# A fused attention, MLP and soft mixture of experts: g turned by VectorE in 32x32 blocks, and the sum over tokens taken from 32x32 array tiles into four partial sums

## The chip, the cores and the metric

The kernel runs on one core of a Trainium2 chip. The metric is the time of one execution on the device in microseconds (us), less being better. The kernel before was timed three times: 657.53, 661.55 and 662.04 us, median 661.55. One more execution was profiled; all rows below are from that one.

TensorE does the matmuls, VectorE (DVE), ScalarE (ACT) and GpSimd (POOL) the elementwise work, and SyncE (SP) issues the DMA transfers.

## The reference

Causal attention over 4 batches of 12 heads (448 tokens, head size 64), then an MLP with a gate, then a soft mixture of experts over all 1792 tokens:

```python
scores = np.where(mask, -1e9, scale * q @ k.T)
attn = exp(scores - max) / sum
x = (attn @ v)                       # 1792 x 768
h = x @ w_in                         # 1792 x 2048
g = h * np.clip(h + 3.0, 0.0, 6.0) / 6.0
y = g @ w_out                        # 1792 x 768
logits = y @ phi                     # 1792 x 32
d = softmax over the tokens of logits
slot_input = d.T @ y                 # 32 x 768, 8 experts x 4 slots
slot_out[e] = np.maximum(slot_input[e] @ w1[e], 0.0) @ w2[e]
out = softmax over the slots of logits @ slot_out
```

## The kernel before

The kernel never forms y. It folds w_out and phi into one matrix wp (2048 x 32), so that the logits come from g, and it takes the slot inputs as U times w_out, where U is the sum over tokens of z (the exponentials of the logits, 32 slots) times g.

Attention runs over 24 pairs of heads, six to a batch. A pair has first score matmuls for the maxima (L473, in two parts, with mask matmuls L479), the maxima on VectorE (L488 and L492), a small matrix from them (the diagonal, L502 to L506, on POOL or VectorE), the masked matmuls into PSUM (L523 and L528, two parts), the exponentials on ScalarE (L538), and the product with v (L561). Both kinds of scores take their PSUM buffers from one pool, "ps".

The MLP's hidden layer is done in f-tiles of 128 features: for each batch 16 groups of 18 matmuls (L731), with the weights prepared by L717 and L720. ScalarE forms the gate (L736) and VectorE multiplies (L738), which gives g with features on the partitions, 128 x 448. The logits take it as it is (L760 and L779). The sum over tokens needs the tokens on the partitions, so TensorE transposes each f-tile of g in four pieces (L745) and ScalarE copies them into the tile gtok in two (L750 and L752). When a batch is complete, its z is transposed (L871; of the last batch L807) and 16 matmuls with K = 128 tokens, M = 32 slots and N = 512 features form its part of U on four column tiles of the array (L889; of the last batch L831, in four quarters), and VectorE adds it to U with the factor by which the running maximum has changed (L900, L837).

After the last batch, U is transposed (L994, L996) and multiplied with w_out (L1004), the slot inputs go through selb (L1021), and eight experts' weights w1 and w2 (64 loads of 768 KB into buffers of a pool called ring, and into parts of the tile wos) are used as they arrive (L1051 and on). Last, the combine and the output.

The order of all instructions is worked out by a planner (class Schedule) from costs, priorities and the buffers of each pool that are free. In a pool outside of SHARED, buffers are handed out in the order in which the code asked for them; in a SHARED one (here "t" and "h") whoever is ready takes one. Each engine then runs its list in order. The weights' ring buffers appear step by step, when earlier memory is given back: cv_end, a_end, b_end, x_end, h_end (after the last hidden group), g_end (after every user of the pools "g", "r" and "ls"), m_end, o_end (after the slot inputs' last matmul). Table RINGS says how many buffers each step adds. SyncE has one list for all of this, so a load that waits holds the ones behind it.

Of the kernel before, what the change touches and what calls it, by code (L numbers as in the profile page):

```python
# [19 lines left out]
TU = {'PO': [-6.32, -14.01, -12.03, 3.38], 'TO': [-7.42, -13.26, 43.39, 23.92], 'PB': 0.63, 'AB': -1.38, 'TB': 194.0, 'DUTY': 0.6, 'RINGS': [2, 4, 2, 3, 1, 6, 2, 3], 'LOOK': 0.49, 'FILL': 0.96, 'RAW': 3, 'CA': 1, 'CW': 1, 'S': 2, 'PAIR': 13.04, 'UNIT': 5.54, 'WP0': 36.34, 'WPS': 13.71, 'T0': 215.5, 'L0': 24.86, 'L1': 5.94, 'GP': 198.33, 'TP': 5.85, 'ZP': 54.85, 'UP': 15.88, 'P0': 15.72, 'NQ': 2, 'WAIT': 0.09, 'AHEAD': 2.19, 'LAT': 0.23, 'CX': 2, 'G': 5, 'R': 1, 'VR': 2, 'XT': 2, 'Q': 1, 'AS': 1.42, 'A1': -6.49, 'A2': 8.66, 'A3': 15.93, 'A4': -8.97, 'A5': 11.2, 'A6': 28.01, 'A7': 15.62, 'DG': 2, 'DV': 6, 'TT': 2, 'LO': 5.3, 'DA': 6, 'DX': 6}  # L20
# [17 lines left out]
class Schedule:  # L38
# [4 lines left out]
    LAT = 0.15  # L43
# [8 lines left out]
    SHARED = ("t", "h")  # L52
# [14 lines left out]
    def buf(self, name):  # L67
        b = Buf(name)
        self.queue.setdefault(name, []).append(b)
        return b  # L70
# [17 lines left out]
    def ready_at(self, s):  # L88
        t = max([d.end + self.LATS.get(d.eng, 0.0) for d in s.deps], default=0.0)
        need = {}  # L90
        for b in s.use:
            if b.t is None:
                if b.pool not in self.SHARED and self.queue[b.pool][0] is not b:
                    return None
                need[b.pool] = need.get(b.pool, 0) + 1
# [22 lines left out]
    def run(self):  # L118
# [8 lines left out]
        while todo:  # L127
# [28 lines left out]
            for b in s.use:  # L156
                if b.t is None:
                    fr = min(self.free[b.pool], key=lambda x: x[:2])
                    self.free[b.pool].remove(fr)
                    self.queue[b.pool].remove(b)  # L160
# [25 lines left out]
def kernel(  # L186
# [81 lines left out]
    with tc.manual_schedule():  # L268
# [58 lines left out]
        sc.pool("zt", [zt])  # L327
# [362 lines left out]
        SM, SNM, SAL, SSUM, SB, SMN = 0, 1, 2, 3, 4, 5  # L690
# [9 lines left out]
        for b in range(B):  # L700
# [5 lines left out]
            for ft in range(KF):  # L706
# [34 lines left out]
                tp = sc.buf("t")  # L741
# [12 lines left out]
                a = sc.add("PE", 0.47, tr, [gg], [tp, g, gtb], pr - TU["TP"])  # L754
                a.weight = 0.35
                lasts.append(sc.add("ACT", 0.75, ev, [a], [tp, gtb], pr - TU["GP"]))
                if ft == KF - 3 if fin and ft > KF - 4 else ft % 4 == 3:
# [9 lines left out]
                    ll = sc.add("PE", 0.9, lg, gts[-nx:] + [wp_done[ft // 4]], [L] + gs[-nx:], pr - TU["TP"])  # L767
            pr = T0 + UNIT * KF - TU["ZP"]
# [6 lines left out]
            if fin:  # L775
# [465 lines left out]
```

## Time and profile before

| | |
|---|---|
| median of three runs | 661.55 us |
| profiled execution, span | 659.1 us |
| TensorE busy | 608.8 us (92%), 5800 instructions |
| VectorE busy | 391.5 us (59%) |
| ScalarE busy | 281.7 us (43%) |
| POOL busy | 144.9 us (22%) |
| moved by DMA | 144.57 MB, mean 219 GB/s |

The profile gives each instruction's start and duration, by line of the kernel. Busy time over the whole span says little here, since the kernel has stages with different limits; it has to be read by stretch. The chain that ended last is followed back from the last instruction through what released each one. Instructions of TensorE are pipelined, so that a single duration is longer than the distance between two. A matmul of 32-bit operands appears as two instructions in the trace.

### The profile page before, as it was taken

To read this page: it belongs to the slowest core of one execution; us is meant where nothing else is said; L and a number is where in the kernel's file an instruction comes from. 1 tells how busy PE (TensorE), PEld (TensorE's weight loads), DVE (VectorE), ACT (ScalarE), POOL (GpSimd) and SP (SyncE) were. 2 spreads that over 40 slices of the span, in tenths; PEclk is the share of its full clock that TensorE was granted. 3 is DMA by queue.
4 is the path that set the end of the run, shared out by engine and by line. 5 is a ranking of instruction groups with operands and counts; after the bars stand their busy time and mean duration, and the time that the engine had idled before them with its cause. 6 is when DMAs were issued, how large, how long until landed. Compare 5 with 4: busy or idle time off the path is not lost.

```text
span 659.1 us, 14610 instructions
## 1 busy us (share of the span) xinstructions
PE 608.8 (92%) x5800; PEld 460.3 (70%) x5800; DVE 391.5 (59%) x900; ACT 281.7 (43%) x518; POOL 144.9 (22%) x199
## 2 busy tenths in 40 slices
PE   7799878989998989999999999999999999999682
PEld 5677756878775866888887788887788854555131
DVE  5698767988888866775667877445333334001022
ACT  2356635655653544554445355454244521110022
POOL 1234505466445311122222113100000001000000
PEclk9699979999997999999999999999999999998897
DMA  7699778979987788655664563435992379999996
GB/s 201 201 311 295 213 230 238 249 169 224 284 188 202 180 204 234 127 118 125 132 140 91 114 137 87 96 79 134 384 370 74 119 269 408 414 415 413 391 319 195
DMA packets 196243, 144.57 MB, mean 219 GB/s; under 512 B 154704, under 2 KB 174672, under 8 KB 196176
## 3 DMA queue, kind: packets, MB, share of 16 engines
q1 hardware_dynamic: 196176, 143.66, 74.0%
q8 instruction: 45, 0.74, 0.5%
q14 instruction: 22, 0.18, 0.1%
HBM read 121.41 MB, written 22.22 MB: 218 GB/s over the span
## 4 chain that ended last, share of the span: by engine, by line
PE 50%; DMA 16%; DVE 8%; SPq 2%; issue 2%; ACT 2%; DVEq 0%; ACTq 0%
PE ph L731 22%; DMA ring<-in_moe_w_dram 9%; PE pl L731 7%; PE t L745 4%; PE ps L523 3%; PE o L561 3%; DVE ps L488 2%; DMA xt<-xd 2%; PE o L1158 2%; SPq L403 2%; PE ps L473 2%; DMA wos<-in_moe_w_dram 1%; PE t L889 1%; DMA raw<-in_moe_w_in_dram 1%; DMA xd<-xt 1%
## 5 line engine op out<-in xcount | busy, mean ns | idle before, releaser
L731 PE MATMUL ph<-xp,wpl 128*128 128x448 f32 x846 | 184.2, 371 | 0.0
L731 PEld LDWEIGHTS ph<-xp,wpl 128*128 128x128 f32 x846 | 155.6, 188 | 19.8 <-issue 4.5
L546 POOL TENSOR_SCALAR_AFFINE_SELECT s<-s 128x256 f32<-128x256 f32 x96 | 49.8, 542 | 180.2 <-ACT s L538 175.5
L736 ACT ACTIVATE r<-ph,three 128x448 f32<-128x448 f32 x47 | 29.8, 634 | 101.4 <-PE ph L731 101.3
L488 DVE CUSTOM_DVE_ANT_0 ps<-ps,maskw 128x448 f32<-128x448 f32 (+3 forms) x144 | 61.7, 429 | 17.5 <-PE ps L473 13.8
L731 PE MATMUL pl<-xp,wpl 128*128 128x448 f32 x306 | 68.5, 377 | 0.1
L738 DVE SCALAR_TENSOR_TENSOR g<-r,ph 128x448 f32<-128x448 f32 x47 | 29.0, 617 | 60.1 <-ACT r L736 60.1
L731 PEld LDWEIGHTS pl<-xp,wpl 128*128 128x128 f32 x306 | 57.5, 192 | 7.5 <-issue 2.2
L523 PE MATMUL ps<-qp,kp 64*64 64x64 f32 (+3 forms) x576 | 57.5, 306 | 5.2 <-ACT s L538 5.2
L722 POOL TENSOR_TENSOR wpl<-cx,wpl 128x768 fp32r<-128x768 f32 x24 | 46.0, 1918 | 56.4 <-ACT wpl L717 56.4
L523 PEld LDWEIGHTS ps<-qp,kp 64*128 64x128 f32 (+1 forms) x576 | 41.9, 175 | 21.8 <-issue 9.4
L717 ACT ACTIVATE wpl<-cx 128x768 fp32r<-128x768 f32 x64 | 53.6, 838 | 7.4 <-DVE cx L636 7.1
L561 PE MATMUL o<-vr,s 128*64 128x65 f32 (+1 forms) x1536 | 55.5, 228 | 0.3 <-POOL s L546 0.3
L538 ACT ACTIVATE s<-ps 128x896 f32<-128x896 f32 (+2 forms) x72 | 50.0, 730 | 13.3 <-PE ps L528 13.1
L561 PEld LDWEIGHTS o<-vr,s 128*64 128x64 f32 (+1 forms) x1536 | 50.3, 141 | 6.0 <-issue 3.4
L720 DVE TENSOR_TENSOR wpl<-cx,wpl 128x768 fp32r<-128x768 f32 x40 | 39.0, 974 | 14.9 <-ACT wpl L717 12.7
L750 ACT ACTIVATE gtok<-t 128x384 f32<-128x384 f32 x64 | 31.1, 486 | 35.1 <-PE t L745 35.0
L624 ACT ACTIVATE ca<-raw 128x768 f32<-128x768 f32 x32 | 29.3, 916 | 37.9 <-DMA raw<-in_moe_w_out_dram 15.8
L473 PE MATMUL ps<-kp,qp 64*128 64x448 f32 (+1 forms) x192 | 27.6, 347 | 14.7 <-DVE mc L488 6.6
L745 PE MATMUL t<-ident,g 128*128 128x128 f32 (+1 forms) x256 | 38.8, 283 | 1.7 <-DVE g L738 1.7
L633 DVE SCALAR_TENSOR_TENSOR cw<-ca,cw 128x768 uint32<-128x768 uint32 x32 | 34.1, 1065 | 2.4 <-ACT ca L624 1.5
L745 PEld LDWEIGHTS t<-ident,g 128*128 128x128 f32 (+1 forms) x256 | 26.9, 134 | 10.5 <-DVE g L738 2.9
(220 smaller groups left out, 806.5 us busy)
## 6 DMA issues: line engine op xcount, KB each, us to landing
ring<-in_moe_w_dram SPq DMA_DIRECT2D x54, 768.0 KB, 12.3
cx<-wi_d SPq DMA_DIRECT2D x48, 384.0 KB, 3.4
raw<-in_moe_w_out_dram SPq DMA_DIRECT2D x16, 768.0 KB, 6.9
raw<-in_moe_w_in_dram SPq DMA_DIRECT2D x16, 768.0 KB, 6.9
wos<-in_moe_w_dram SPq DMA_DIRECT2D x10, 768.0 KB, 14.2
wo_d<-gtok SPq DMA_DIRECT2D x16, 384.0 KB, 4.3
wi_d<-cx SPq DMA_DIRECT2D x16, 384.0 KB, 5.1
wos<-wo_d SPq DMA_DIRECT2D x16, 384.0 KB, 6.1
```

The source lines that it names most:

```text
L473: nc.tensor.matmul(ps.t[:n, h, c:c + w], pl["q"].t[r, 0, q0:q0 + n], pl["k"].t[r, 0, 0:w], start=(t == part[0][0]), stop=adds, skip_group_ ...
L488: nc.vector.tensor_tensor_reduce(out=x, in0=x, in1=maskw[:n, 320 - q0:320 + n] if t else maskw[:n, 320:320 + n], scale=-1.0, scalar=3.0e38 ...
L523: nc.tensor.matmul(ps.t[:kn, h, col:col + n], pl["k"].t[r, x, q0:q0 + kn], pl["q"].t[r, y, q0:S], start=(c == 0 and col == 0), stop=False, ...
L538: nc.scalar.activation(out=o, in_=x, func=ACTF.Exp, scale=SCALE)
L546: nc.gpsimd.affine_select(out=x, in_=x, pattern=[[0, 2], [1, kn]], compare_op=ALU.is_ge, fill=0.0, base=0, channel_multiplier=-1)
L561: nc.tensor.matmul(o.t[64 * h:64 * h + 64, VD * j:VD * j + VD], s.t[:kn, h, c:c + 64], vr.t[:kn, h, t, :], start=(t == 0), stop=(t == ts[- ...
L633: e = sc.add("DVE", 1.04, lambda: nc.vector.scalar_tensor_tensor(out=cw.t, in0=ca.t.bitcast(U32), scalar=3, in1=cw.t, op0=ALU.logical_shif ...
L717: e = sc.add("ACT", 0.84, lambda w=w, cx=cx: nc.scalar.activation(out=w.t[:, 0], in_=cx.t, func=ACTF.Copy), [cr], [cx, w], ps_)
L720: ("DVE", 1.0, lambda w=w, cx=cx: nc.vector.tensor_sub(w.t[:, 1], cx.t, w.t[:, 0].bitcast(F32))),
L722: ("POOL", 2.0, lambda w=w, cx=cx: nc.gpsimd.tensor_sub(w.t[:, 1], cx.t, w.t[:, 0].bitcast(F32))),
L731: nc.tensor.matmul(h.t[:, :S], w.t[:, a, kk, :], x.t[:, c, kk, :], start=(n == 0), stop=(n == len(seq) - 1))
L745: nc.tensor.transpose(tp.t[:n, t * P:(t + 1) * P], g.t[:, t0:t0 + n], ident)
```

## The change

Six edits:

1. g of batches 1 to 3 is turned by one VectorE transpose per f-tile, which turns each block of 32x32 in place and leaves the blocks where they are. TensorE's transposes and ScalarE's copies stay for batch 0 alone.
2. The sum over tokens of batches 1 to 3 therefore has K = 32 tokens of a block, M = 32 slots, N = 512, on 16 tiles of the array: four row groups, each into its own PSUM bank (two of pool "t" and both halves of one of "ps"). z is turned by VectorE too. VectorE adds the four banks into a new tile U4 that keeps the four parts apart.
3. At the end the parts are added by matmuls (L1042 with U of batch 0, whose factor SAL0 is put into a scaled identity idS, and L1046 with U4), in eight steps, in place of L994. idS is taken from the pool "g". The slot inputs are formed in eight halves (L1059), in a buffer of pool "o" and not "ps".
4. "ps" becomes SHARED.
5. The tile zt becomes a buffer of memory that is given back with g; U4 takes 8 KB more in each partition.
6. RINGS begins with 1, not 2.

```diff
-    SHARED = ("t", "h")
+    SHARED = ("t", "h", "ps")
...
+                if b:
+                    lasts.append(sc.add("DVE", 0.64, lambda g=g, ft=ft: nc.vector.transpose(
+                        gflat[:, ft * S:(ft + 1) * S], g.t), [gg], [g, gtb], pr - TU["GP"]))
+                tp = None if b else sc.buf("t")
...
-                a = sc.add("PE", 0.47, tr, [gg], [tp, g, gtb], pr - TU["TP"])
-                a.weight = 0.35
-                lasts.append(sc.add("ACT", 0.75, ev, [a], [tp, gtb], pr - TU["GP"]))
+                if not b:
+                    a = sc.add("PE", 0.47, tr, [gg], [tp, g, gtb], pr - TU["TP"])
+                    a.weight = 0.35
+                    lasts.append(sc.add("ACT", 0.75, ev, [a], [tp, gtb], pr - TU["GP"]))
...
+            def ublocks(banks, zT):
+                for j in range(S // 32):
+                    for i in range(4):
+                        r = slice(32 * i, 32 * i + 32)
+                        o = 32 * (j % 4)
+                        nc.tensor.matmul(
+                            banks[i][o:o + 32, :], zT.t[r, 32 * j:32 * j + 32], ug[r, :, 32 * j:32 * j + 32],
+                            start=(j < 4), stop=(j + 4 >= S // 32), tile_position=(32 * i, o),
+                        )
...
+                zT, idS = sc.buf("zT"), sc.buf("g")
+                zd = sc.add("DVE", 0.64, lambda: nc.vector.transpose(zT.t, z.t), [zz], [z, zT], T1)
...
+                um = sc.add("PE", 3.7, lambda: ublocks(banks(), zT), [zd] + lasts, [gtb, zT, u2] + ub, T1)
...
+                    def uadd(cs=cs):
+                        for i in range(4):
+                            nc.vector.scalar_tensor_tensor(
+                                out=U4[:, cs, i], in0=U4[:, cs, i], scalar=c1(SAL), in1=blk(banks()[i])[:, cs],
+                                op0=ALU.mult, op1=ALU.add)
...
+                def utr(up=up, c=c, j0=j0):
+                    nc.tensor.matmul(
+                        up.t[:, :64], U[:, c * P:(c + 1) * P], idS.t[:, 32 * j0:32 * j0 + 64],
+                        start=True, stop=False, skip_group_check=True)
+                    for j in range(2):
+                        nc.tensor.matmul(
+                            up.t[:, 32 * j:32 * j + 32], U4[:, 4 * (j0 + j) + c].rearrange("p i x -> p (i x)"),
+                            sel4[:, 0, :], start=False, stop=(j == 1), skip_group_check=True)
```

How the planner's order moves, at three places. In the rows, a name's number tells buffers apart, and lines of the changed kernel are three higher in the first half (L473 becomes L476, L523 becomes L526, L528 becomes L531, L403 becomes L406).

TensorE at the start of attention, the second pair's first scores and the first pair's masked matmuls. Before:

```order
L443 MATMUL t_261<-ident,kr_224 128x112 x4
L387 MATMUL ph_255<-ident 32x128 x4
L523 MATMUL ps_258<-qp_231,kp_233 128x448 x6
L528 MATMUL ps_258<-dg_241,oner 128x448 x2
L523 MATMUL ps_258<-qp_231,kp_233 64x64 x6
L528 MATMUL ps_258<-dg_241,oner 64x64 x2
```

Now:

```order
L446 MATMUL t_258<-ident,kr_221 128x112 x4
L390 MATMUL ph_252<-ident 32x128 x2
L476 MATMUL ps_255<-kp_231,qp_229 128x448 x2
L482 MATMUL ps_255<-maskr,halfr 128x128 x2
L482 MATMUL ps_255<-maskr,halfr 128x64 x2
L476 MATMUL ps_255<-kp_231,qp_229 64x64 x2
L482 MATMUL ps_255<-maskr,halfr 64x64 x2
L390 MATMUL ph_252<-ident 32x128 x3
L526 MATMUL ps_255<-qp_228,kp_230 128x448 x6
L531 MATMUL ps_255<-dg_238,oner 128x448 x2
```

A first score part of the next pair (L476) now stands ahead of the masked matmuls (L526). In the whole of TensorE's list, the products with v of 16 pairs now stand ahead of batch 0's sum over tokens, where there were 13, and 19 hidden groups stand ahead of it in both.

TensorE after the last hidden group, from the sum over tokens to the slot inputs. Before:

```order
L831 MATMUL ph_256<-gtok,zt 32x128 x16
L831 MATMUL pl<-gtok,zt 32x128 x16
L994 MATMUL t_260<-ident,U 128x128
L831 MATMUL ph_255<-gtok,zt 32x128 x16
L1004 MATMUL ps_258<-wos,wp 32x384 x8
L994 MATMUL t_261<-ident,U 128x128
L994 MATMUL t_260<-ident,U 128x128
L831 MATMUL ph_256<-gtok,zt 32x128 x16
L1004 MATMUL ps_258<-wos,wp 32x384 x8
L994 MATMUL t_261<-ident,U 128x128
L1004 MATMUL ps_258<-wos,wp 32x384 x16
```

Now, from the last of 42 rows of the sum over tokens (56 matmuls, L785) on; g_196 is the scaled identity:

```order
L785 MATMUL ps_255<-gtok,zT_199 32x512 x2
L390 MATMUL o_256<-ident 32x128 x2
L1042 MATMUL ph_252<-g_196,U 128x64
L1046 MATMUL ph_252<-sel_74,U_82 128x32 x2
L1042 MATMUL ph_253<-g_196,U 128x64
L1046 MATMUL ph_253<-sel_74,U_82 128x32 x2
L1042 MATMUL pl<-g_196,U 128x64
L1046 MATMUL pl<-sel_74,U_82 128x32 x2
L1059 MATMUL o_256<-wos,wp 32x384 x4
L1042 MATMUL ph_252<-g_196,U 128x64
L1046 MATMUL ph_252<-sel_74,U_82 128x32 x2
L1059 MATMUL o_256<-wos,wp 32x384 x4
```

The sum over tokens is one piece. Three combining steps follow, then one half of the slot inputs, then four times a step and a half; the eighth step and the last three halves come last. Before, the quarters of the sum alternated with transposes and slot inputs.

SyncE's list, from the ring load of x_end to the last of m_end (the five loads into wos come next). Before:

```order
L403 DMA ring_5811<-in_moe_w_dram 128x1536
L403 DMA ring_5848<-in_moe_w_dram 128x1536
L403 DMA ring_5852<-in_moe_w_dram 128x1536
L403 DMA ring_5856<-in_moe_w_dram 128x1536
L403 DMA ring_5860<-in_moe_w_dram 128x1536
L403 DMA ring_5864<-in_moe_w_dram 128x1536
L403 DMA ring_5868<-in_moe_w_dram 128x1536
L403 DMA ring_5920<-in_moe_w_dram 128x1536
L403 DMA ring_5924<-in_moe_w_dram 128x1536
L403 DMA ring_6042<-in_moe_w_dram 128x1536
L403 DMA ring_6046<-in_moe_w_dram 128x1536
L403 DMA ring_6050<-in_moe_w_dram 128x1536
```

Now:

```order
L406 DMA ring_5680<-in_moe_w_dram 128x1536
L406 DMA ring_5712<-in_moe_w_dram 128x1536
L406 DMA ring_5716<-in_moe_w_dram 128x1536
L406 DMA ring_5720<-in_moe_w_dram 128x1536
L406 DMA ring_5724<-in_moe_w_dram 128x1536
L406 DMA ring_5728<-in_moe_w_dram 128x1536
L406 DMA ring_5732<-in_moe_w_dram 128x1536
L406 DMA ring_5829<-in_moe_w_dram 128x1536
L406 DMA ring_5833<-in_moe_w_dram 128x1536
L406 DMA ring_5859<-in_moe_w_dram 128x1536
L406 DMA ring_5863<-in_moe_w_dram 128x1536
L406 DMA ring_5867<-in_moe_w_dram 128x1536
```

The order of the steps is the same: one load of x_end, six of h_end, two of g_end, three of m_end. What each waits for has moved. Before, ring_5848 waited for a weight preparation (L720), the five behind it for the last hidden group, ring_5920 for the transposes of z (L807) and the exponentials (L795), ring_6042 for the last sum over tokens (L831). Now all of 5712 to 5732 wait for the last hidden group, and ring_5829 waits for the eighth L1042, the last reader of the scaled identity; 5833 to 5867 stand behind it. Before the first of these rows, 12 loads into ring buffers stood in the list counting ring_5811; now 11 do counting ring_5680.

## Rows read from the trace of the kernel before

**Rows 1.** Busy time by stretch of the span; columns in the first line, us.
```profile
core 0: us, PE busy (x) PEld busy (x) DVE busy (x) ACT busy (x) POOL busy (x), PEclk, DMA share, GB/s
0.00:259.60 259.60, 233.31 (x2596) 186.18 (x2598) 205.88 (x418) 135.11 (x227) 103.72 (x145) 0.95 0.84 228
259.60:533.30 273.70, 271.79 (x2277) 223.82 (x2278) 160.39 (x400) 125.33 (x246) 39.42 (x53) 1.00 0.56 144
533.30:550.50 17.20, 16.02 (x234) 7.71 (x236) 5.40 (x20) 3.60 (x9) 1.27 (x1) 1.00 0.95 367
550.50:629.30 78.80, 72.64 (x632) 35.41 (x624) 10.71 (x46) 8.41 (x17) 0.53 (x1) 0.89 1.02 408
```

**Rows 2.** Chain that ended last, 259.6 to 533.3 us, shares by line.
```profile
by line: PE ph L731 49.5%; PE pl L731 12.2%; PE t L745 8.2%; PE o L561 7.1%; PE ps L523 6.9%; PE ps L473 3.3%; PE t L889 2.7%; PE pl L760 2.3%; PE ps L528 1.9%; PE ph L760 1.3%; DVE ps L488 1.2%; PE t L772 0.8%; issue 0.5%; DVE wpl L720 0.4
```

**Rows 3.** Matmuls by line, 259.6 to 533.3 us; xcount | busy us, mean ns | idle before.
```profile
L731 PE MATMUL ph<-xp,wpl 128*128 128x448 f32 x648 | 141.2, 371 | 0.0
L745 PE MATMUL t<-ident,g 128*128 128x128 f32 (+1 forms) x184 | 27.1, 279 | 0.4 <-DVE g L738 0.4
L561 PE MATMUL o<-vr,s 128*64 128x65 f32 (+1 forms) x704 | 24.5, 224 | 0.0
L889 PE MATMUL t<-gtok,zt 128*32 128x512 f32 (+1 forms) x64 | 7.5, 597 | 0.0
```

**Rows 4.** Timeline of one attention pair; start us, us, engine, line, instruction.
```profile
38.90 0.47 PE L473 MATMUL ps<-kp,qp 64*128 64x448 f32 x2
43.21 1.28 DVE L492 TENSOR_REDUCE mc<-ps 128x2 f32<-128x384 f32 x2
45.41 0.94 POOL L506 TENSOR_TENSOR dg<-id,mc 128x448 fp32r<-128x448 f32 x1
46.74 0.88 PE L523 MATMUL ps<-qp,kp 64*128 64x448 f32 x6
52.69 0.47 PE L473 MATMUL ps<-kp,qp 64*128 64x448 f32 x2
```

**Rows 5.** Timeline of SyncE: issues of weight loads around H.
```profile
527.26 0.33 SPq L403 DMA_DIRECT2D ring<-in_moe_w_dram  x1
539.66 0.33 SPq L403 DMA_DIRECT2D ring<-in_moe_w_dram  x1
546.69 1.28 SPq L403 DMA_DIRECT2D ring<-in_moe_w_dram  x3
550.45 2.35 SPq L403 DMA_DIRECT2D wos<-in_moe_w_dram  x5
```

**Rows 6.** VectorE by line and shape, whole span.
```profile
L601 DVE STREAM_TRANSPOSE tx<-xt 128x448 f32<-128x448 f32 x18 | 11.6, 644 | 19.5 <-DMA xt<-xd 19.4
L900 DVE SCALAR_TENSOR_TENSOR U<-U,st,t 128x512 f32<-128x512 f32 x2 | 1.5, 740 | 1.4 <-PE t L889 1.4
L837 DVE SCALAR_TENSOR_TENSOR U<-U,st,ph 128x128 f32<-128x128 f32 x3 | 1.0, 347 | 2.0 <-PE ph L831 2.0
```

**Rows 7.** Timeline after H.
```profile
533.97 0.62 DVE L738 SCALAR_TENSOR_TENSOR g<-r,ph 128x448 f32<-128x448 f32 x1 [3.87 <-ACT r L736]
535.90 0.96 PE L779 MATMUL t<-g,wp 128*32 128x448 f32 x8
536.93 0.53 ACT L786 ACTIVATE r<-t 32x448 f32<-32x448 f32 x1
537.49 0.62 DVE L790 TENSOR_REDUCE st<-t 128x1 f32<-128x448 f32 x1 [2.90 <-ACT r L786]
538.40 0.63 ACT L795 ACTIVATE ls<-t,st 128x448 f32<-128x448 f32 x1 [0.94 <-DVE st L791]
538.93 0.19 ACT L795 ACTIVATION_READ_ACCUMULATOR ls<-t,st 128x1 f32 x1
546.56 1.50 PE L1004 MATMUL ps<-wos,wp 128*32 128x384 f32 x16
551.98 1.26 PE L1021 MATMUL t<-selb,wos 128*128 128x64 f32 x6 [0.31 <-ACT wos L1017]
```

**Rows 8.** DMA issues of the whole span, from the page; count, size, us to landing.
```profile
ring<-in_moe_w_dram SPq DMA_DIRECT2D x54, 768.0 KB, 12.3
```

More of the change, by code (lines that the diff above doesn't have):

```diff
@@ L65, in grant, with buf @@
         self.free[name].append((self.now, len(self.free[name]) + 100, tile))
-    def buf(self, name):
+    def buf(self, name, ordered=True):
         b = Buf(name)
-        self.queue.setdefault(name, []).append(b)
+        b.ordered = ordered and name not in self.SHARED
+        if b.ordered:
+            self.queue.setdefault(name, []).append(b)
         return b
@@ L92, in ready_at @@
             if b.t is None:
-                if b.pool not in self.SHARED and self.queue[b.pool][0] is not b:
+                if b.ordered and self.queue[b.pool][0] is not b:
                     return None
@@ L159, in run @@
                     self.free[b.pool].remove(fr)
-                    self.queue[b.pool].remove(b)
+                    if b.ordered:
+                        self.queue[b.pool].remove(b)
                     b.slot, b.t = fr[1:]
@@ L866, with uadd @@
             prev_stat = sc.add("DVE", 0.15, stat, [zz], [], pr)
+            if b:
+                logits_out(lt, [a2], pr)
+                zT = sc.buf("zT")
+                zd = sc.add("DVE", 0.64, lambda z=z, zT=zT: nc.vector.transpose(zT.t, z.t), [zz], [z, zT], pr)
+                ub, u2 = [sc.buf("t") for _ in range(2)], sc.buf("ps", False)
+                banks = lambda ub=ub, u2=u2: [ub[0].t, ub[1].t, u2.t[:, 0], u2.t[:, 1]]
+                a = sc.add("PE", 3.7, lambda banks=banks, zT=zT: ublocks(banks(), zT), [zd] + lasts,
+                           [gtb, zT, u2] + ub, T0 + UNIT * KF - TU["UP"])
+                def uadd(b=b, banks=banks):
+                    for i in range(4):
+                        if b == 1:
+                            nc.vector.tensor_copy(U4[:, :, i], blk(banks()[i]))
+                        else:
+                            nc.vector.scalar_tensor_tensor(
+                                out=U4[:, :, i], in0=U4[:, :, i], scalar=c1(SAL), in1=blk(banks()[i]),
+                                op0=ALU.mult, op1=ALU.add)
+                prev_u = sc.add("DVE", 2.5, uadd, [a, prev_stat, prev_u], ub + [u2], pr)
+                prev_stat = prev_u
+                continue
             tp = sc.buf("t")
```

115 lines of the change are left out of this document (55 added, 60 removed).

## The prediction

> **What bounds the kernel now.** I first read busy time by stretch [rows 1]. There the reader is to see three kernels in one. Up to 259.6 us, where batch 0's sum over tokens ends, TensorE is busy for 233.3 of 259.6 us, VectorE for 79% and the DMA engines for 84%: each waits a little for the others, and TensorE idles for 26.3 us. From 259.6 to 533.3 TensorE is busy for 271.8 of 273.7 us, so what is taken from TensorE there comes off the time. From 533.3 on (H below: the end of the last hidden group, L731) the DMA engines are the limit: 408 GB/s at a share of 1.02 from 550.5 to 629.3, while weights of the experts stream in. Second, the chain that ended last in the middle stretch, by line [rows 2]: L745, the TensorE transposes of g, has 8.2% of it. Third, single durations [rows 3, 4, 6, 7]. Fourth, when SyncE issues the weight loads after H [rows 5].
>
> **The middle stretch.** L745 stands there 184 times [rows 3], four per f-tile, so for 46 of the 48 f-tiles of batches 1 to 3; the last two are turned after H. Its share of the chain is 8.2% of 273.7 = 22.4 us, 0.49 per f-tile. All 46 go. What replaces each is one VectorE transpose of 128x448, which the trace has at 644 ns on another tile [rows 6]: 46 x 0.644 = 29.6 us, so VectorE rises from 160.4 to 190 of some 251 us, 76%: hidden behind the matmuls of the next f-tile. ScalarE loses its two copies per f-tile; it isn't the limit, so this is worth nothing. The sum over tokens of a batch is 32 instructions in 3.75 us now [rows 3]: four column tiles at once, eight passes of 0.47 us. The new one has 56 matmuls, thus 112 instructions, on 16 tiles. Do the row groups of 32 overlap too? Nearest is L523, whose matmuls lie in two row groups of 64: six of 448 columns take 0.88 us [rows 4], 0.15 each, where a hidden matmul of 448 columns, alone on the array, takes 3.9/18 = 0.22 (L731's 648 instructions are 36 f-tiles of 18 in 141.2 us [rows 3]). So two row groups run side by side; four were not seen. If all overlap, the fullest column tile takes 4 x 2 = 8 passes, 3.8 us as before; in pairs, 14 x 0.47 = 6.6; one after another, 28 x 0.47 = 13.2. I take 3.9, nearest to the row that does overlap. Three such sums: +0.4 at most, +8.5 with pairs, +28 without. With some 0.5 for the two sums in this stretch and for matmuls that now wait for banks, the stretch gives **-21.5**.
>
> The Trainium skill (TensorE: Matmul & The Clock Gate, Part 3, packing small matmuls) gives a measured 10.6 times for 16 tiles of K = M = 32 against 3.07 for four, so not a full fourfold gain. By that, as an estimate, the sum takes 3.75 x 112/32 x 3.07/10.6 = 3.8 us; the sixteenfold reading would give 3.3. No row here has 16 tiles; the page speaks against the rival of row groups that queue, and the sum would change by 0.1.
>
> **The early stretch.** The change also makes the PSUM pool "ps" one whose buffers are taken in any order, and the planner uses it: the next pair's first score part is placed ahead of the last pair's masked matmuls, and 16 instead of 13 pairs stand ahead of batch 0's sum over tokens. On the chain of the middle stretch the attention lines L561, L523, L473 and L528 have 19.2% [rows 2], 52.6 us for some 10.5 pairs (L561's 704 instructions are 11 pairs of 64 [rows 3]), 5.0 per pair. So 15 us of TensorE work moves from the middle stretch into the early one. What it costs there I bound twice. From above: all of it fits into the 26.3 idle us [rows 1], and the end comes 15 earlier. From below by the cadence: from one pair's first scores to the next, L473 at 38.90 to L473 at 52.69, is 13.79 us [rows 4], and in it TensorE waits for the diagonal: the last maximum ends at 44.49, POOL's diagonal at 46.35, the masked matmuls start at 46.74, a gap of 2.25 us. With scores of the next pair already placed in it, it may go. If it goes wholly, 16 pairs at 11.54 take 184.6 us where 13 took 179.3: +5.3 - 15 = -10. If half goes, 16 at 12.66 take 202.6: +23.3 - 15 = +8. Between -15 and +8 I take **-3**: TensorE is 90% busy already, and VectorE, which does each pair's maxima, 79%.
>
> **After H.** Counted from H = 533.3, by the order of the changed kernel. The last g is ready at +1.3 (533.97 + 0.62 [rows 7]). Its logits (0.96) no longer wait behind L745, and end at +2.5; the copy (0.53) ends at +3.1; maximum and negation, 0.91 from the start of L790 to the start of L795, end at +4.0; exp and its sum end at +4.8 (now: 539.12, +5.8). VectorE turns z: +5.5. The sum over tokens, 112 instructions, no longer in quarters: +9.4. Then VectorE adds four banks, in two halves of 4 instructions of 128x256: between 347 ns at 128 columns and 740 at 512 [rows 6], 0.48 each, so the first half is there at +11.3, the second at +13.2. Eight new combining steps follow (L1042 and L1046, 3 matmuls with 128x128 weights, 6 instructions; the like, L1021, takes 1.26 for six and follows at 0.173 each [rows 7], so 1.05), with eight halves of the slot inputs, L1059, 0.75 each (half of 1.50 [rows 7]). Three combining steps to +14.4, one half to +15.2, four pairs of 1.80 to +22.4, a third of the eighth step: **+22.7**. All eight read a scaled identity that sits in a buffer of pool "g", and the release of "g" waits for every user. So the next weight loads (ring_5829 on, and three more behind it on SP's queue) wait until +22.7. Now that release goes at 539.66, +6.4, and the following at 546.69, +13.4 [rows 5]. The matmuls themselves end at +25.9, where they end near +17.1 now (550.45 [rows 5]).
>
> What that costs: a load is 768 KB [rows 8], 0.786 MB at 408 GB/s = 1.93 us. Six loads stand ahead of the held one, 11.6 us of transfers. Now the same 17.2 us at 367 GB/s lose 17.2 x (1 - 367/408) = 1.7 to the start. The start is lost again; then the engines are idle from +13.3 to +22.7 and start anew with 1.7: 9.4 + 1.7 = 11.1. Beside it fewer loads are done at H: one ring buffer less at the beginning, and the first of the six, which now goes at 527.26, waits for the last hidden group: 11 of 64 done instead of 13, 2 x 1.93 = 3.9. Together **+15.0**. Between +6 (the add and the combining steps overlapped twice as well) and +20 (steps one after another, and a lower clock: 0.89 was granted at 550.5 to 629.3 [rows 1]).
>
> **Sum.** -21.5 - 3 + 15.0 = -9.5; 659.1 - 9.5 = 649.6 us of span. The median of the runs, 661.55, is 2.45 above the profiled span, so **652**.
>
> **The rivals.**
> One: as summed, 646 to 658. 0.42.
> Two: the early stretch takes the three pairs for nothing, -15: 652 - 12 = 640. For it speaks the idle time there, against it VectorE and DMA at 79 and 84%. 0.17.
> Three: the early stretch is held by its cadence with VectorE and DMA, half of the gap stays: 652 + 11 = 663. Or the pairs only change places, 655. For it: the three engines near 80 to 90% at once. 0.17.
> Four: the loads held back after H do not matter, since something else sets the end: 652 - 15 = 637. Against it stand 78.8 us at the full rate [rows 1]. 0.06.
> Five, on the other side: row groups of 32 do not run side by side, and each of the three sums takes 13.2 instead of 3.8: 652 + 28 = 680, slower. In pairs, 660. It decides from about 9.3 us per sum on (16 more in all). Nothing shows four at once; L523 shows two. 0.08, half of it for pairs.
> Six: VectorE becomes the limit in the middle stretch. The maxima of attention, g and the weight differences share it; were each of the 45 turns to hold up a hidden group by 0.3 us, 652 + 13 = 665. At 76% busy this isn't likely. 0.10.
>
> **Numbers.** About 1% is what a measurement of this kernel can tell from no change: 654.9 and 668.2 are the bounds. Faster: four fifths of case one (0.34), two (0.17), four (0.06): 0.57, shortened to 0.56. Same: the rest of one (0.08), three (0.17), six (0.09), pairs of five (0.04): 0.37. Slower: the rest, 0.07. The range: leave out four below and the slow half of five above, and the ends of two and six: 638 to 666. Case one alone has 646 to 658.
>
> **What would show it.** Right is: no L745 on TensorE after batch 0 except as VectorE transposes of about 0.64 us; the stretch from batch 0's sum to H shorter by 21.5 + 15 = 36 us; the end of batch 0's sum 12 us later; a new sum over tokens of 3.8 to 4.1 us; the first load behind the release of "g" 22 to 23 us after H, and before it some 9 us in which the DMA engines are empty; then 408 GB/s to the end. Wrong would be: gaps of TensorE in the middle stretch that end with VectorE; a sum over tokens of more than 6 us; DMA engines that stay busy through the 20 us after H; or batch 0's sum earlier than 265 us or later than 285.

## The result

The changed kernel takes 660.06 us in the median of 20 runs, the kernel before 657.28 in the median of 20: a ratio of 1.0058, 95% interval 1.0031 to 1.0085. That is within 1%, on the slow side; 652 was forecast. One kernel's executions scatter by 12 to 13 us (650.8 to 663.6 for the kernel before, 656.1 to 668.1 for the changed one), so that a profiled execution is a sample: that of the changed kernel has a span of 656.1 us and lies low among its runs, that of the kernel before, 659.1, lies high among its own. Both kernels were therefore profiled a second time, and the terms below are read from two executions each. The ratios compare undisturbed executions alone, so that one can differ from that of the medians beside it.

Busy time by stretch, the changed kernel, cut as in [rows 1]: at the end of batch 0's sum over tokens, at the last hidden group (H = 518.8), at the first load into wos, and where the weights are in. The columns are as there.

```profile
0.00:283.40 283.40, 253.65 (x2946) 201.80 (x2946) 224.10 (x512) 148.24 (x248) 104.08 (x162) 0.96 0.84 220
283.40:518.80 235.40, 233.78 (x1931) 193.23 (x1932) 149.04 (x329) 85.80 (x134) 48.35 (x61) 1.00 0.54 149
518.80:542.20 23.40, 20.90 (x258) 11.14 (x257) 8.62 (x28) 2.26 (x6) 1.80 (x1) 1.00 0.59 217
542.20:626.30 84.10, 71.62 (x614) 34.63 (x616) 10.72 (x46) 8.40 (x17) 0.00 (x0) 0.90 1.02 409
626.30:656.10 29.80, 17.75 (x76) 8.60 (x72) 9.21 (x17) 9.23 (x21) 0.00 (x0) 0.85 0.80 263
```

The middle stretch is 38.3 us shorter than in [rows 1], the early one 23.8 longer, the part after H 137.3 us and not 125.8. Here are the second profiles, the kernel before first, the changed kernel in the next fence. That of the kernel before was expected to show 17.2 us from H to the first load into wos again, and does.

```profile
0.00:254.10 254.10, 230.38 (x2596) 183.90 (x2596) 209.08 (x419) 135.79 (x227) 105.61 (x145) 0.97 0.85 234
254.10:526.70 272.60, 271.64 (x2281) 223.87 (x2278) 159.42 (x399) 124.82 (x244) 39.45 (x53) 1.00 0.55 145
526.70:543.90 17.20, 16.02 (x235) 7.78 (x237) 5.41 (x20) 3.60 (x9) 1.20 (x1) 1.00 0.95 368
543.90:651.80 107.90, 87.91 (x700) 42.78 (x692) 19.94 (x63) 17.73 (x38) 0.61 (x1) 0.89 0.95 365
```

```profile
0.00:282.80 282.80, 253.43 (x2946) 201.14 (x2948) 221.14 (x511) 148.38 (x248) 104.77 (x162) 0.96 0.85 220
282.80:518.00 235.20, 233.66 (x1931) 193.19 (x1932) 149.06 (x330) 85.82 (x134) 48.48 (x61) 1.00 0.54 149
518.00:548.50 30.50, 28.12 (x249) 14.73 (x251) 8.61 (x28) 2.26 (x6) 1.80 (x1) 0.70 0.46 167
548.50:662.40 113.90, 90.32 (x704) 43.84 (x696) 19.92 (x63) 17.64 (x38) 0.00 (x0) 0.89 0.97 371
```

| us | before, two executions | changed, two executions | difference of the means | forecast |
|---|---|---|---|---|
| to the end of batch 0's sum | 259.6, 254.1 | 283.4, 282.8 | +26.3 | +12 |
| from there to H | 273.7, 272.6 | 235.4, 235.2 | -37.9 | -36.5 |
| from H to the first load into wos | 17.2, 17.2 | 23.4, 30.5 | +9.8 | +9 |
| the rest | 108.6, 107.9 | 113.9, 113.9 | +5.7 | +6 |
| span | 659.1, 651.8 | 656.1, 662.4 | +3.8 | -9.5 |

(The forecast of +12 is -3 with the 15 us of the three pairs; of -36.5, -21.5 with the same 15 taken out; the last two split the +15.0.) The difference of the spans agrees with that of the medians, +2.8. One row is far from its forecast, the first. The others lie nearer than their terms: the second is a sum of two errors that cancel, and 3.5 of the +9.8 in the third are a lower clock in one of the two executions (both below).

TensorE in the middle stretch of the changed kernel, by line, as [rows 3]:

```profile
L734 PE MATMUL ph<-xp,wpl 128*128 128x448 f32 x414 | 89.7, 370 | 0.0
L564 PE MATMUL o<-vr,s 128*64 128x65 f32 (+1 forms) x512 | 17.9, 224 | 0.0
L785 PE MATMUL t<-gtok,zT 32*32 32x512 f32 x112 | 9.1, 597 | 0.0
L785 PE MATMUL ps<-gtok,zT 32*32 32x512 f32 x112 | 8.6, 598 | 0.0
```

No transposes of g are left there, and 8 pairs (512/64) stand where there were 11. What replaced them, on VectorE over the whole span:

```profile
L745 DVE STREAM_TRANSPOSE gtok<-g 128x448 f32<-128x448 f32 x48 | 29.8, 633 | 4.0 <-PE ps L785 3.1
```

48 turns at 633 ns, where [rows 6] led to 644. After H, the timeline of the changed kernel (some rows of the sum over tokens, the first addition, the first and the eighth combining step, and SyncE):

```profile
524.18 0.62 PE L785 MATMUL t<-gtok,zT 32*32 32x512 f32 x2 [0.95 <-DVE zT L840]
...
524.28 0.62 PE L785 MATMUL ps<-gtok,zT 32*32 32x512 f32 x2
524.63 0.59 PE L785 MATMUL t<-gtok,zT 32*32 32x512 f32 x2
...
527.90 0.61 PE L785 MATMUL ps<-gtok,zT 32*32 32x512 f32 x2
528.50 0.87 DVE L857 SCALAR_TENSOR_TENSOR U<-U,st,t 128x256 f32<-128x256 f32 x2 [3.52 <-PE ps L785]
529.00 0.43 PE L1042 MATMUL ph<-g,U 128*128 128x64 f32 x2
...
539.16 0.43 PE L1042 MATMUL ph<-g,U 128*128 128x64 f32 x2
539.63 2.54 SPq L406 DMA_DIRECT2D ring<-in_moe_w_dram  x5
...
542.21 4.43 SPq L406 DMA_DIRECT2D wos<-in_moe_w_dram  x5
```

Each of the 56 f32 matmuls of the sum is two instructions (the 18 matmuls of a hidden group, with operands of the type fp32r, are 18). Sixteen instructions start within 0.1 us of each other (524.18 to 524.28, eight rows of two) and the next sixteen from 524.63 on, so the four row groups run side by side, and the sum takes 4.3 us (524.18 to 528.5). The held loads go at 539.63, H + 20.8, where those of [rows 5] went at H + 6.4 and H + 13.4, and before that the DMA engines are empty, which one stretch shows (last two columns: share, GB/s):

```profile
532.00:540.00 8.00, 8.00 (x76) 4.63 (x79) 1.12 (x5) 0.00 (x0) 1.80 (x1) 1.00 0.03 12
```

### The profile page after: what moved, and what is told of

Read it like the earlier page. It is cut to its first block, busy times and chain, and to the rows that moved or that the text cites. A ratio compares the mean times of both kernels' runs of the same rounds, so it can differ in the third digit from the quotient of the medians.

```text
span 656.1 us, 14652 instructions
## 1 busy us (share of the span) xinstructions
PE 597.7 (91%) x5820; PEld 449.4 (68%) x5820; DVE 401.7 (61%) x931; ACT 253.9 (39%) x426; POOL 154.2 (24%) x223
## 4 chain that ended last, share of the span: by engine, by line
PE 41%; DMA 14%; DVE 4%; SPq 2%; ACT 1%; issue 1%; DVEq 0%; ACTq 0%
PE ph L734 13%; PE pl L734 12%; DMA ring<-in_moe_w_dram 10%; PE o L564 3%; DMA wos<-in_moe_w_dram 2%; PE ps L526 2%; SPq L406 2%; PE ph L767 1%; PE t L785 1%; DVE ps L491 1%; DMA xt<-xd 1%; PE o L1213 1%; PE ps L476 1%; PE ps L1243 1%; PE ps L785 1%
## 5 line engine op out<-in xcount | busy, mean ns | idle before, releaser
L734 PE MATMUL ph<-xp,wpl 128*128 128x448 f32 x738 | 162.6, 373 | 0.8 <-DVE wpl L723 0.8
L734 PEld LDWEIGHTS ph<-xp,wpl 128*128 128x128 f32 x738 | 137.5, 190 | 18.8 <-issue 4.8
L734 PE MATMUL pl<-xp,wpl 128*128 128x448 f32 x414 | 90.3, 371 | 0.0
L734 PEld LDWEIGHTS pl<-xp,wpl 128*128 128x128 f32 x414 | 76.4, 188 | 14.0 <-issue 4.6
L720 ACT ACTIVATE wpl<-cx 128x768 fp32r<-128x768 f32 x64 | 53.5, 838 | 33.0 <-PE pl L734 9.2
L526 PE MATMUL ps<-qp,kp 64*64 64x64 f32 (+3 forms) x576 | 57.8, 307 | 9.2 <-DVE mc L495 4.0
L739 ACT ACTIVATE r<-ph,three 128x448 f32<-128x448 f32 x41 | 25.9, 633 | 94.1 <-PE ph L734 92.3
L526 PEld LDWEIGHTS ps<-qp,kp 64*128 64x128 f32 (+1 forms) x576 | 42.1, 175 | 24.2 <-issue 6.2
L741 DVE SCALAR_TENSOR_TENSOR g<-r,ph 128x448 f32<-128x448 f32 x41 | 25.2, 615 | 31.7 <-ACT r L739 31.4
L627 ACT ACTIVATE ca<-raw 128x768 f32<-128x768 f32 x32 | 29.4, 918 | 32.2 <-DMA raw<-in_moe_w_in_dram 14.5
L723 DVE TENSOR_TENSOR wpl<-cx,wpl 128x768 fp32r<-128x768 f32 x38 | 35.6, 937 | 7.1 <-ACT wpl L720 6.7
L476 PE MATMUL ps<-kp,qp 64*128 64x448 f32 (+1 forms) x192 | 27.6, 345 | 13.0 <-ACT s L541 6.5
L739 ACT ACTIVATE r<-pl,three 128x448 f32<-128x448 f32 x23 | 14.6, 633 | 60.2 <-PE pl L734 60.2
L1213 PE MATMUL o<-ring,wos 128*32 128x384 f32 x216 | 28.4, 534 | 6.4 <-DMA ring<-in_moe_w_dram 6.4
L745 DVE STREAM_TRANSPOSE gtok<-g 128x448 f32<-128x448 f32 x48 | 29.8, 633 | 4.0 <-PE ps L785 3.1
```

What stands on the lines that cost most here:

```text
L476: nc.tensor.matmul(ps.t[:n, h, c:c + w], pl["q"].t[r, 0, q0:q0 + n], pl["k"].t[r, 0, 0:w], start=(t == part[0][0]), stop=adds, skip_group_ ...
L526: nc.tensor.matmul(ps.t[:kn, h, col:col + n], pl["k"].t[r, x, q0:q0 + kn], pl["q"].t[r, y, q0:S], start=(c == 0 and col == 0), stop=False, ...
L720: e = sc.add("ACT", 0.84, lambda w=w, cx=cx: nc.scalar.activation(out=w.t[:, 0], in_=cx.t, func=ACTF.Copy), [cr], [cx, w], ps_)
L723: ("DVE", 1.0, lambda w=w, cx=cx: nc.vector.tensor_sub(w.t[:, 1], cx.t, w.t[:, 0].bitcast(F32))),
L734: nc.tensor.matmul(h.t[:, :S], w.t[:, a, kk, :], x.t[:, c, kk, :], start=(n == 0), stop=(n == len(seq) - 1))
L739: rr = sc.add("ACT", 0.63, lambda h=h, r=r: nc.scalar.activation(out=r.t, in_=h.t[:, :S], func=ACTF.Relu, bias=three), [hh], [h, r], pr - ...
```

## The experiments

**One part alone, in the kernel before: "ps" in any order.**

```diff
-    SHARED = ("t", "h")
+    SHARED = ("t", "h", "ps")
```

> The kernel before with one edit: "ps" is SHARED. TensorE's list gets the 16 pairs ahead of batch 0's sum over tokens, with nothing else of the change. Theory A: batch 0's sum ends some 24 us later than before, the middle stretch is 15 us shorter: 8 to 9 us more, ratio 1.013. Theory B (neutral order): 1.000. As I predicted the early stretch: 3 us less, 0.995.

Measured: 668.28 us, ratio 1.0149 (1.0092 to 1.0206). Its stretches:

```profile
0.00:286.40 286.40, 254.61 (x2946) 202.01 (x2946) 220.62 (x511) 148.04 (x248) 103.85 (x161) 0.96 0.84 217
286.40:540.20 253.80, 251.21 (x1953) 209.87 (x1954) 127.07 (x299) 114.57 (x226) 34.24 (x42) 1.00 0.52 145
540.20:557.30 17.10, 16.14 (x236) 7.95 (x239) 5.40 (x20) 3.59 (x9) 1.14 (x1) 1.00 0.95 364
```

This is theory A. Against the means of the two executions of the kernel before, the early stretch is 29.5 us longer and the middle one 19.4 shorter; what the three pairs cost early is more than they give later. So a pair is worth 6.5 us in the middle stretch, not the 5.0 of the prediction, and costs 9.8 in the early one. From here to the changed kernel the middle stretch falls by another 18.4 us (253.8 to 235.4), which is what the turned g and the new sum give.

**The other part alone: "ps" in order, the rest of the change as it is.**

```diff
-    SHARED = ("t", "h", "ps")
+    SHARED = ("t", "h")
```

> The changed kernel with the pool "ps" handed out in order as before; all else of the change stays. TensorE's list then has 13 pairs ahead of batch 0's sum over tokens again, as before, and not 16. Theory A (the moved pairs cost the early stretch more than they save later): batch 0's sum ends near 260 us again, the stretch from there to the last hidden group is about 22 us shorter than before (274 to 252), the part after it 11 us longer: ratio to before near 0.984. Theory B (the order of attention is neutral; the expected gain is lost in the middle stretch, to VectorE or to PSUM banks): the time stays that of the changed kernel, 1.006.

Measured: 667.93 us, ratio 1.0118 (1.0067 to 1.0169). Neither theory: the early stretch is as before, but the gain in the middle stretch is lost too.

```profile
0.00:260.70 260.70, 234.66 (x2596) 187.59 (x2596) 210.32 (x420) 135.47 (x227) 102.68 (x146) 0.95 0.83 225
260.70:526.30 265.60, 261.70 (x2332) 215.34 (x2332) 181.63 (x442) 96.25 (x152) 53.52 (x59) 1.00 0.56 146
```

265.6 us where 252 was expected. The lines of TensorE say where the rest is: of the 22 us of L745 only 7 to 8 came off (273.7 and 272.6 to 265.6), and 88 filler instructions stand there now (the larger group is shown), which the planner puts where it sees TensorE waiting.

```profile
L390 PE MATMUL ph<-ident 128*32 128x128 f32 x72 | 9.0, 275 | 0.0
```

In the kernel before, sharing "ps" costs 1.5%. With g turned by VectorE it does not: the changed kernel, which shares it, is at 1.006 and 1.007, against 1.012 here. The intervals overlap, so a gain is not shown. That sharing does no harm there because it takes three pairs out of a stretch that TensorE no longer holds is an argument; no run tests it alone.

**The fillers taken out of that kernel's middle stretch.**

```diff
+        hold = []
...
         def filler(t0, t1):
+            if hold:
+                return
...
+                        hold.clear()
...
+                hold.append(1)
```

> As the run with "ps" in order (1.012), but the planner puts no filler matmuls (L390) between batch 0's sum over tokens and the last hidden group; that run had 88 filler instructions there, 11.5 us of TensorE. Theory A (the fillers stand where TensorE would have waited for attention's maxima and exponentials): the stretch stays near 266 us, now with about 10 us of visible idle time that VectorE or ScalarE ends: ratio near 1.012 again. Theory B (the fillers themselves take the time that the transposes gave back): the stretch falls to about 254 us, ratio near 0.995.

Measured: 680.87 us, ratio 1.0356 (1.0297 to 1.0415). The fillers did not take the time. Without them TensorE idles openly and its clock falls: the stretch takes 286.5 us, at a mean granted clock of 0.94 where every other kernel here has 0.99 or 1.0.

```profile
256.00:542.50 286.50, 265.83 (x2243) 216.01 (x2244) 180.81 (x443) 96.84 (x155) 56.23 (x61) 0.94 0.52 135
```

Theory A holds in that TensorE idles (20.7 us, where about 10 was expected), and errs as to the time, since it left the clock out.

**"ps" in order for the first 13 pairs, then in any order; no scaled identity.**

```diff
-                ps = sc.buf("ps")
+                ps = sc.buf("ps", i < 13)
...
```

The same edit stands at both places where a pair takes a buffer of "ps", and the scaled identity goes as in the run without it below.

> No scaled identity, and "ps" in order for the first 13 pairs alone, in any order for the other 11. Batch 0's sum again stands behind 13 pairs and ends near 260 us. Theory A (with 11 pairs left, the middle stretch is held by VectorE's and ScalarE's part of attention, whatever the buffers' order): the stretch is near 265 us as in the run with "ps" in order, ratio near 1.003. Theory B (the buffers' order was what held it): the stretch is near 252 us, ratio near 0.975.

Measured: 668.35 us, ratio 1.0153 (1.0098 to 1.0208); the middle stretch takes 272.7 us.

```profile
0.00:257.10 257.10, 235.24 (x2598) 188.08 (x2598) 208.31 (x426) 133.44 (x225) 105.08 (x144) 0.97 0.84 228
257.10:529.80 272.70, 259.56 (x2313) 213.99 (x2310) 177.30 (x410) 97.26 (x156) 61.92 (x87) 1.00 0.55 142
```

Neither figure came (265 or 252 us), but the order of the buffers is not what held the stretch. From the end of batch 0's sum to the last product with v, the kernel before takes 187.1 us for 11 pairs, the one with "ps" in order 192.5, this one 178.3, and the changed kernel 141.0 for 8: 16 to 18 us a pair in each. A pair of attention passes hardly faster because L745 is gone. Which engine sets this pace was not separated; VectorE is busy for 69 to 75% of these four spans of time.

**What sets the early stretch: less work for VectorE, or fewer bytes.** The first leaves out the low bits of the weights:

```diff
-                out=cw.t, in0=ca.t.bitcast(U32), scalar=3, in1=cw.t,
+                out=cw.t[:, 0:1], in0=ca.t[:, 0:1].bitcast(U32), scalar=3, in1=cw.t[:, 0:1],
```

> The changed kernel with one of the four steps that unpack the weights (L636, 32 times 0.98 us on VectorE, all of it ahead of batch 0's sum over tokens) done on a sixth of its columns, so that the low bits of the weights are left out; the order of every engine stays. About 26 us less of VectorE's 224 us in the early stretch. Theory V (VectorE's work sets the early stretch, so that a moved pair brings about 8 us and not the 5 of TensorE): batch 0's sum ends 15 to 26 us earlier than at 283 us. Theory D (the DMA engines, at a share of 0.84, set it): it ends within 3 us of 283.

The second leaves out half of the weights:

```diff
-            l = sc.load(0.79e6, lambda: dma(raw.t.rearrange("p k f t -> p k (f t)"), src), [], [raw], prio - 12)
+            l = sc.load(0.79e6, lambda: dma(raw.t.rearrange("p k f t -> p k (f t)")[:, 0:3], src[:, 0:3]), [], [raw], prio - 12)
```

> The changed kernel with half of each of the 32 loads of 768 KB that bring the packed weights left out (the tiles are zeroed once at the start); the order of the engines stays. 12.6 MB less of some 62 MB that are moved in the early stretch. Theory D: batch 0's sum ends 15 us or more before 283 us, and VectorE's 20.7 us of waiting for these loads go. Theory V: it ends within 5 us of 283, since the waits for loads only move to other places.

Measured, one execution of each, the early stretch of the one and of the other:

```profile
0.00:279.80 279.80, 253.64 (x2946) 202.19 (x2947) 201.25 (x512) 148.34 (x248) 99.08 (x162) 0.96 0.86 222
```

```profile
0.00:266.00 266.00, 247.60 (x2946) 197.78 (x2946) 223.98 (x511) 147.22 (x248) 111.42 (x165) 0.99 0.74 185
```

VectorE lost 20 to 23 us of work, and the stretch 3 to 4 us, which is less than executions differ by: four executions whose early stretch is the same (two of the changed kernel, one each of the kernels without the scaled identity and with matmuls in the two waits, below) end it between 282.8 and 288.8 us. The DMA engines lost 12.6 MB, and the stretch 17 us, with VectorE's work unchanged at 224 us: 11 of them are TensorE's idle time (29.8 to 18.4 us) and 6 its busy time, at a granted clock of 0.99 and not 0.96. So theory D is the nearer one, within limits. The DMA engines' own time fell by about 41 us (0.84 of 283.4 to 0.74 of 266.0), of which 17 came back, so they are not all that sets the stretch. And what was taken away are large transfers: packets under 512 B are still 106 thousand. VectorE's waits for these loads (L630 for both weight tensors, 20.7 us in the changed kernel, the first two rows) nearly go (the last two):

```profile
DVE cw L630 <- DMA raw<-in_moe_w_in_dram: 13.2, 8, 2.8
...
DVE cw L630 <- DMA raw<-in_moe_w_out_dram: 7.5, 4, 2.6
```

```profile
DVE cw L631 <- DMA raw<-in_moe_w_out_dram: 2.3, 2, 1.2
...
DVE cw L631 <- DMA raw<-in_moe_w_in_dram: 1.3, 2, 1.0
```

A moved pair brings its own transfers, and they are small. The DMA packets of the early stretch, of the kernel before (to 259.6 us) and of the changed one (to 283.4):

```profile
DMA packets 103887, 59.29 MB, mean 228 GB/s; under 512 B 83898, under 2 KB 96186, under 8 KB 103857
```

```profile
DMA packets 127427, 62.24 MB, mean 220 GB/s; under 512 B 107551, under 2 KB 119839, under 8 KB 127390
```

3 MB more, but 23.5 thousand packets more, nearly all under 512 B, at a share of 0.84 in both. That is some 20 us more of the DMA engines' time, and 22 in the mean of both pairs of executions. TensorE's busy time rises by as much, from 233.3 and 230.4 us to 253.7 and 253.4, but 5 to 6 of these 21.7 us are fillers (L387 and L390).

**The held loads: no scaled identity.** VectorE scales U of batch 0 in place, and nothing in pool "g" is read by the combining steps.

```diff
-                s0 = sc.add("DVE", 0.2, lambda: nc.vector.tensor_scalar_mul(idS.t[:, 0:P], ident, c1(SAL0)), [s0], [idS], T1 + 1)
+                s0 = sc.add("DVE", 0.35, lambda: nc.vector.tensor_scalar_mul(U, U, c1(SAL0)), [s0, prev_u], [], T1 + 1)
...
-                        up.t[:, :64], U[:, c * P:(c + 1) * P], idS.t[:, 32 * j0:32 * j0 + 64],
+                        up.t[:, :64], U[:, c * P:(c + 1) * P], ident[:, 32 * j0:32 * j0 + 64],
```

> The changed kernel without the scaled identity: VectorE scales U of batch 0 in place and the combining matmuls read the plain identity, so that nothing in pool "g" is read by them. Theory A (the weight loads held until the eighth combining step set the end): the first held load goes some 9.5 us after the last hidden group and not 20.8, the 8 us in which the DMA engines were empty and the new start of 1.7 go: 9 to 10 us less than the changed kernel, ratio to before near 0.991. Theory B (the end is set by something else, such as the length of TensorE's tail): the time stays, 1.006.

Measured: 653.28 us, ratio 0.9931 (0.9891 to 0.9972). Theory A, though with 7 to 8 us less than the changed kernel and not 9 to 10: the five held loads go at H + 9.8 (521.1 to 530.86), and seven of twelve runs lie at 651 to 654 us. The profiled execution was one of the other five, at 658.17, and shows something else: 17.1 us, in the combining steps, in which TensorE's clock was granted at 0.50 (1.2 GHz).

```profile
530.86 2.25 SPq L406 DMA_DIRECT2D ring<-in_moe_w_dram  x5
```

```profile
535.20:552.30 17.10, 16.84 (x90) 8.49 (x86) 1.27 (x6) 0.00 (x0) 1.80 (x1) 0.50 0.77 283
```

**Both edits, "ps" in order and no scaled identity.**

> Both edits: "ps" in order as before, and no scaled identity. If both theories A hold and the two parts add, 22 us less in the middle stretch and about 1.5 more after the last hidden group: ratio to before near 0.969. If only the attention order counts, 0.984; if only the loads, 0.991; if neither, 1.006.

Measured: 662.63 us in the median of twelve runs from 649 to 671. The ratio of 0.9889 (0.9829 to 0.9949) is that of two of them alone, 649.26 and 654.78; the medians of all would give 1.006. The middle stretch of the profiled execution takes 268.3 us, as with "ps" in order alone, and the clock fell after H (a mean of 0.72 from H to 560 us). With times so far apart it does not tell the four expectations apart.

**The changed kernel a second time, for the clock.**

> The changed kernel once more, for a second profile. If the clock in the combining steps is what parts the times, then a profile with a clock of 0.5 there has a stretch from the last hidden group to the first load into wos that is some 6 to 8 us longer than the 23.4 us of the first profile, and one without has 23 to 24 us. Otherwise the difference between two executions lies before the last hidden group.

Measured: 662.03 us, ratio 1.0073 (1.0039 to 1.0106). Up to H the two profiles differ by 0.8 us. After H the second has the clock at 0.50 for 17.1 us, from 533.6 on, and the first load into wos at H + 30.5 and not + 23.4:

```profile
533.60:550.70 17.10, 17.04 (x90) 8.58 (x86) 1.12 (x5) 0.00 (x0) 1.80 (x1) 0.50 0.23 75
```

A shorter fall to 0.50 stands ahead of this one, from 523.3 to 526.6, in the sum over tokens, which takes 5.8 us there and not 4.3. So 7 us between the two executions are the clock after H, 1.6 of them in the sum over tokens and 5.5 from the combining steps on. The kernel before has its sum over tokens in quarters between its transposes, and in neither of its profiles does the clock fall there ([rows 1] and the second profile: 1.00 in these 17 us).

**Matmuls in the two waits after H.** Without the scaled identity, and with two matmuls of 128x448, read by nobody, while the exponentials are made, and two while the banks are added.

```diff
+                            nc.tensor.matmul(kb.t[:, :448], ident, wp.rearrange("p a s -> p (a s)")[:, 0:448], start=True, stop=True)
...
+                keep(2, [a2], T1 + 2)
...
+                keep(2, [um], T1 - 1)
```

> No scaled identity, as in the run at 0.993, and two matmuls of 128x448 with 128x128 weights, whose result nobody reads, in each of two places after the last hidden group where TensorE has nothing to do: while the exponentials are made, and while the four banks are added. Theory A (in the profiled execution of 0.993 TensorE's clock was granted at 0.5 for 17.1 us from the combining steps on, and this is what parts its times into 651 to 654 and 658 to 665 us): the clock stays at 1.0 there, and all times are near the lower group: median 651 to 653 us, ratio 0.988 to 0.991. Theory B (the spread comes from the early stretch): median and spread stay.

Measured: 650.01 us, ratio 0.9876 (0.9844 to 0.9908), eleven of twelve runs from 646 to 655 us. As theory A has it, the clock is 1.00 from H to the first load into wos, which goes at H + 19.0. One profile can't show that the four matmuls did this, since three of the nine profiled executions that end in this way without them have no fall either (last section).

```profile
524.20:543.20 19.00, 18.10 (x213) 9.29 (x211) 8.37 (x26) 2.26 (x6) 1.59 (x1) 1.00 0.96 376
```

**Larger packets for three pairs**, on top of this kernel (two entries of its table TU).

```diff
-'DV': 6
-'DX': 6
+'DV': 9
+'DX': 9
```

> The run at 0.988 (no scaled identity, busy tail) with one more edit: DV and DX are 9, not 6, so that TensorE, and not loads in pieces of 128 bytes, turns q and k of pairs 6 to 8 of the planner's numbering, and their outputs do not go to memory and back to be turned. Between 114 and 250 us the changed kernel moved 72611 packets, 59801 of them under 512 B, in 83% of the DMA engines' time. Theory D (the DMA engines' time sets the early stretch; such a pair takes them some 7 us, of which about 5 go): the last hidden group ends 8 to 15 us earlier, near 510 us, ratio 0.966 to 0.976. Theory P (TensorE, which gets 2 us more work per pair and is at 90%, takes the place): the time stays, 0.988.

Measured: 645.43 us, ratio 0.9781 (0.9729 to 0.9834): the fastest here, and faster than both kernels. The ratio lies between theory D (0.966 to 0.976) and theory P (0.988), nearer to D. H is at 516.1, 8 us before that of the last kernel and 2 to 8 us before the 518.0 to 524.2 of the four profiles that share the changed kernel's early order. The planner's order moved as well: 13 pairs and 17 hidden groups stand ahead of batch 0's sum now, so that the two stretches can't be set against the others one by one, and the gain is not shown to be that of the packets.

```profile
0.00:236.80 236.80, 219.97 (x2622) 177.74 (x2622) 193.10 (x417) 128.36 (x219) 91.13 (x137) 0.96 0.84 237
236.80:516.10 279.30, 268.94 (x2347) 221.89 (x2344) 178.77 (x419) 101.77 (x161) 59.70 (x83) 0.99 0.55 143
```

## Why the prediction was wrong

**The middle stretch: right in its mechanisms, and near in size by luck.** -36.5 was forecast with the three pairs, -37.9 measured. With "ps" shared in the kernel before, the pairs alone take 19.4 us from this stretch where 15 was forecast, and the turned g and the new sum then take 18.4 where 21.5 was: two errors that cancel. The pairs were sized at 5.0 us each by their lines' share of the chain, and moving them out gave 6.5. Why the turned g gave 3 us less than L745's share of the chain stays open, but for about 1 us in two sums over tokens of 4.3 us in place of 3.75. VectorE's turns are hidden (it is busy for 149 of 235.4 us), the sum over tokens takes 4.3 us where 3.9 was taken and 13.2 was the other bound, and TensorE is busy for 233.8 of 235.4 us. The rivals of queued row groups and of VectorE as the limit both fell. The estimate from the Trainium skill (TensorE: Matmul & The Clock Gate, Part 3), 3.8 us, was near; the trace has sixteen tiles side by side.

**After H: right in mechanism and near in size.** The eighth combining step was forecast at H + 22.7 and its release was seen at + 20.8; 9.4 us of empty DMA engines were forecast and 8 seen; +15.0 was forecast and +11.5 measured in the execution with the full clock (137.3 against 125.8). The edit that takes the wait away gained some 7 to 8 us (660.06 to 653.28 in the medians, 1.006 to 0.993 in the ratios), so that rival four, loads that don't matter, fell. What the step did not see is the clock after H. It named a lower clock only as part of a bound, from another stretch; in the second execution it costs 7 us more. That the two executions together have +15.5 here, next to the forecast of +15.0, is therefore luck.

**The early stretch: the step that failed.** It was sized at -3, from bounds of -15 and +8: three more pairs were to lengthen the stretch by 12 us, since part of them would fill TensorE's idle time and its wait for the diagonal. They lengthened it by 26.3. With the two executions of each kernel the step is +26.3 - 15 = +11, outside its own bounds, and the change of "ps" alone does the same in the kernel before (+29.5 us here, +1.5% of the whole). Two things in it were wrong. First, nothing was filled. TensorE's busy time rose by 21.7 us, 5 to 6 of them fillers, so the pairs' own work came in full on top, 15 to 17 us where 15 was taken. TensorE's idle time, which was to shrink, rose from 26.3 and 23.7 us to 29.8 and 29.4; with the fillers it waited some 10 us more. Second, +8 was no bound: it let half of the gap in front of the masked matmuls go without a row that shows it. With no part of it gone, the cadence of 13.79 us gives 3 x 13.79 = 41 us for three pairs; the 26.3 measured lie between this and the 23.3 of the half.

What sets the stretch is shown in part. Taking 20 to 23 us of work from VectorE gave 3 to 4 us back, within the scatter; taking 12.6 MB from the DMA engines gave 17, 11 of them idle time of TensorE. So part of TensorE's waiting there is, through other engines, for what the DMA engines bring. The prediction had their share of 0.84 among its reasons against rival two, but no term of its sum prices what three pairs add to it. That a pair costs 26.3/3 = 8.8 us, and not the 5 to 6 of its work on TensorE, because it brings the DMA engines some 7 us (about 7850 packets) fits all this, but is argued: no run takes a pair's packets away and keeps the order. Rival two, pairs that fit in for nothing, fell. Rival three, half of the gap staying (663), named the right stretch and nearly the time; of the two engines it blamed beside the cadence, VectorE and DMA, the runs bear out the second.

With +11 in place of -3 the sum would have been +4.5 us of span, and the measured medians differ by +2.8. The chance given to a result within 1% was 0.37.

## What to carry to other kernels

Before work is moved from a stretch that one engine bounds into one that looks loose, price it there by everything it brings. Here a pair brought 5 to 6 us of work for TensorE and some 7 for the DMA engines; it was priced at 5 us of TensorE less what idle time would take up, and it cost 8.8. Idle time of 10% and a mean DMA share of 0.84 were no room; the test is to take bytes away, and work away, and see which gives time back. When a forecast is a sum, check its terms by runs that have one edit each: the middle stretch came out right with two terms wrong. And when a change frees the bound engine, look what holds the same stretch next: here a pair of attention kept its 16 to 18 us, so that with the pairs left in their places only 7 to 8 of the 22 us of L745 came off.

## What the runs showed that was not expected

The clock after H. In one of the two profiled executions of the changed kernel the granted clock is 0.50 (1.2 GHz) for 17.1 us from the combining steps on, and for a shorter time before; in the other it is 1.00 up to the first load into wos. This parts 30.5 from 23.4 us between H and that load. A fall of the same length is in the profiles of five of the other kernels that end in this way, and in two (without the fillers, and with less work for VectorE) there is none. In both executions of the changed kernel TensorE waits twice ahead of this, 0.95 us before the sum over tokens and 0.78 us before the first combining step that needs the added banks, so that the waits alone do not decide it. With matmuls of 128x448 in these two waits it stayed at 1.00 in the profiles of both kernels that had them. Since three of nine executions keep the clock without them, and the cause was not tried apart, their effect rests mainly on the times: eleven of twelve runs at 646 to 655 us, against seven of twelve at 651 to 654 and five at 658 to 665 without these matmuls.
